# Pair 0's products with v begun inside the bias network, and pair 1's first tiles placed ahead of pair 0's last two

## The chip, the core and the metric

The kernel runs on one core of one Trainium2 chip. The metric is the device time of one launch in microseconds (us), from the start of the program to its end. Engines are named as the profile names them: PE is TensorE's matmuls and PEld its weight loads, DVE is VectorE, ACT is ScalarE, POOL is GpSimd, SP is SyncE, whose queue issues nearly all DMAs.

## What is computed

The reference is an attention with a bias made by a small network, followed by a two-layer mixer. Cut to what matters here:

```python
scores = scale * np.matmul(q, k.transpose(0, 1, 3, 2))          # (4, 8, 576, 576), head size 64
x = (psi_rel / psi_i)[..., None]                                # (576, 576, 1): from positions alone
h = np.maximum(x @ w1 + b1, 0.0)                                # 32 hidden values for each pair of positions
bias = h @ w2                                                   # (576, 576, 8): one plane for each head
scores = scores + bias.transpose(2, 0, 1)[None]
attn = np.exp(scores - np.max(scores, axis=-1, keepdims=True))
attn = attn / (np.sum(attn, axis=-1, keepdims=True) + 1e-09)
out = np.matmul(attn, v)                                        # then: u = x + mix(x); u + relu(u @ w1) @ w2
```

## The kernel before

**Two parts matter here: the bias network, and the attention of the 16 pairs that follows it.** A pair `p` is two heads of one batch (4 batches, 4 pairs in each). The last half of the program, the mixer, is not touched.

**The bias network** is the loop at L792, one turn `i` for each of 36 row tiles `T` (16 rows of the bias each), in the order of L786: the four tiles of rows 512 to 575 first, then tiles 0 to 31. In turn `i`, `bias_hid` (L299) makes the four hidden blocks of tile number `i`, mostly one on ACT (L308) and three on DVE (L310). `bias_mm` (L320) then multiplies the hidden blocks of the tile made two turns earlier with w2 on PE (L328), in strips of 32 columns of the array, and `bias_out` (L339) scales the result on ACT (L342) and writes it to DRAM by a DMA (L345). The hidden blocks live in a ring of 12 (three tiles), the scaled results in a ring of 6, and the PSUM tiles tagged `s` in three banks, which scores share. `bias_loads` (L352) reads the finished bias back in the layout of a head pair: `(c, hp)` is row block `c` (0 to 3, or 4 for the last 64 rows) of pair `hp`; `BIAS_AT` and the list `loads` say when.

**A pair** has nine tiles of scores, `s` = 0 to 8. `scores` (L376) puts q k into PSUM (L399), four matmuls of 288 columns, eight for `s` = 0, which holds the last 64 rows of both heads. `minima` (L403) adds the bias and takes the row minimum on DVE (L407), `exps` (L422) is the exponential on ACT (L425). `tr` (L465) transposes a tile on PE (L472) and copies it out as `pt`, `tr_m` (L475) does so for the 64 rows of `s` = 0, `tr_mid` (L484) for the middle columns. `av` (L498) multiplies v with `pt` into one PSUM bank (L508): ten matmuls over 320 columns for the first half `hf` = 0, over 256 for the second. `assemble` (L519) turns the result and scales it. `slot` (L581) puts all of that in order for tile `s` of pair `p`, together with what is left of pair `p` - 1: its last transposes, its second `av`, its `assemble`.

**Pair 0 begins inside the network.** `early` (L788) places the scores of its tiles 0 to 3 in turns 20, 23, 26 and 30; `minima` comes a turn later and the rest of the slot two turns later. Its other five tiles follow the network, then pair 1 and so on, in the loop at L866. The engines are in-order queues: what stands ahead in the program goes first.

**Operands.** q and k are held as two parts each whose sum has full precision: `hi` is the rounded value, and the difference to it goes to the lower half of `hi` for q and to `lo` for k. `prep_ops` (L173) makes them; from pair 1 on this is POOL's work, and POOL does not start it before the last hidden block of the network is written (the copy at L798 waits for it).

## Time and profile before

| | us |
|---|---|
| time, median of 3 runs | 729.47 (728.37 to 730.01) |
| profiled execution, its own time | 727.51 |
| its span, first to last instruction | 725.70 |
| PE busy | 707.5 (97%) |
| DVE busy | 537.1 (74%) |
| ACT busy | 402.9 (56%) |
| POOL busy | 273.1 (38%) |

The span is what the trace shows; the profiled execution is 1.81 us longer than its span, and 1.96 us shorter than the median. The times in brackets in the trace are how long an engine sat idle before an instruction and what released it. A matmul's end is modelled, so the pace of PE is read from the starts, above all from those of the weight loads (PEld). A float32 matmul shows as two records: the ten matmuls of one `av` are 20.

### The profile page before, as it was taken

The numbers are of one execution on the slowest core, as the hardware profiler recorded it, in microseconds if no ns is written. First come the engines' busy times: TensorE is split into PE (matmuls) and PEld (weight loads), VectorE is DVE, ScalarE is ACT, GpSimd is POOL, SyncE is SP. The second block draws the span as 40 slices with busy tenths as digits, with TensorE's granted clock in tenths as the row PEclk, the third lists the DMA queues.
The fourth block names the chain that finished last, engine by engine and source line by source line (L and its number), as shares of the span: only waits on it lengthen the run. The fifth ranks groups of instructions, "written<-read, shape, count | busy, mean of one in ns | idle before, by whom it ended". The sixth has DMA issues, their size and how long they took to land.

```text
span 725.7 us, 13129 instructions
## 1 busy us (share of the span) xinstructions
PE 707.5 (97%) x4620; PEld 561.2 (77%) x4620; DVE 537.1 (74%) x1202; ACT 402.9 (56%) x915; POOL 273.1 (38%) x287
## 2 busy tenths in 40 slices
PE   6999999999999999999999999999999999999997
PEld 2547888788777877878787888888787788888886
DVE  7985688788787777656658689999999953655545
ACT  7897778788778778864223335555555421222220
POOL 0006967567655557701150323536436300000000
PEclk9999999999999999999999999999999999999999
DMA  6889984565565546522293504637434665633313
GB/s 204 272 312 294 304 230 117 140 184 159 140 176 156 144 122 183 182 97 88 74 355 128 206 29 153 217 135 275 149 117 160 239 259 180 256 125 122 155 58 117
DMA packets 53393, 127.19 MB, mean 175 GB/s; under 512 B 8784, under 2 KB 12368, under 8 KB 52048
## 3 DMA queue, kind: packets, MB, share of 16 engines
q1 hardware_dynamic: 53088, 126.10, 53.1%
q8 instruction: 37, 0.61, 0.4%
q10 hardware_dynamic: 240, 0.26, 0.1%
q14 instruction: 28, 0.23, 0.1%
HBM read 81.34 MB, written 44.99 MB: 174 GB/s over the span
## 4 chain that ended last, share of the span: by engine, by line
PE 74%; ACT 9%; DVE 9%; issue 3%; DMA 2%; POOL 2%; SPq 0%; DVEq 0%; POOLq 0%; ACTq 0%
PE po L1334 15%; PE sb L1273 12%; PE o L508 11%; PE sc L399 10%; PE ph L676 7%; PE tb L472 7%; PE po L701 5%; PE bs L328 2%; ACT p L425 1%; POOL wy L266 1%; DVE acc L1320 1%; ACT pt L452 1%; ACT ring L308 1%; PE ph L1362 1%; ACT ring L342 1%
## 5 line engine op out<-in xcount | busy, mean ns | idle before, releaser
L1320 DVE TENSOR_TENSOR acc<-po,acc 128x512 f32<-128x512 f32 x108 | 74.1, 687 | 50.5 <-PE po L1334 44.1
L425 ACT ACTIVATE p<-p,st 128x576 f32<-128x576 f32 x128 | 99.9, 781 | 11.0 <-DVE st L407 10.6
L407 DVE CUSTOM_DVE_ANT_0 p<-sc,bias 128x576 f32<-128x576 f32 x128 | 95.9, 751 | 9.2 <-DMA bias<-bias_dram 4.7
L266 POOL TENSOR_TENSOR wy<-wt,wy 128x256 int32<-128x256 int32 (+1 forms) x68 | 50.3, 740 | 135.4 <-DVE wt L261 118.4
L399 PE MATMUL sc<-hi 128*128 128x288 f32 x320 | 100.6, 331 | 0.1
L399 PE MATMUL sc<-lo,hi 128*128 128x288 f32 x320 | 89.1, 295 | 0.0
L508 PE MATMUL o<-pt,v 128*64 128x320 f32 (+1 forms) x640 | 85.4, 411 | 0.1
L472 PE MATMUL tb<-ident,p 128*128 128x128 f32 x512 | 78.3, 275 | 1.4 <-DVE pt L454 0.9
L1334 PE MATMUL po<-wq,hq 128*128 128x512 f32 x288 | 73.5, 391 | 0.5 <-DVE ut L1367 0.5
L399 PEld LDWEIGHTS sc<-hi 128*128 128x128 f32 x320 | 60.3, 189 | 11.5 <-issue 8.0
L472 PEld LDWEIGHTS tb<-ident,p 128*128 128x128 f32 x512 | 59.8, 140 | 10.9 <-issue 7.6
L508 PEld LDWEIGHTS o<-pt,v 128*64 128x64 f32 x640 | 44.4, 136 | 30.1 <-issue 3.0
L452 ACT COPY pt<-tb 128x512 f32<-128x512 f32 x88 | 51.3, 582 | 23.4 <-PE tb L472 23.2
L1334 PEld LDWEIGHTS po<-wq,hq 128*128 128x128 f32 x288 | 53.5, 188 | 12.6 <-DVE ut L1367 0.9
L399 PEld LDWEIGHTS sc<-lo,hi 128*128 128x128 f32 x320 | 60.6, 189 | 0.5
L1273 PE MATMUL sb<-ut,w1q 128*128 128x512 f32 x216 | 55.1, 390 | 0.4 <-ACT acc L1277 0.3
L1273 PE MATMUL sb<-ut,wq 128*128 128x512 f32 x216 | 55.0, 390 | 0.5 <-ACT acc L1277 0.4
L328 PE MATMUL bs<-ring,small_sb 128*32 128x512 f32 (+48 forms) x640 | 43.8, 400 | 9.2 <-ACT ring L308 6.7
L701 PE MATMUL po<-w2q,hh 128*128 128x512 f32 x216 | 52.2, 393 | 0.4 <-DVE x_sb L576 0.4
L1334 PE MATMUL po<-w2q,ut 128*128 128x512 f32 x180 | 49.1, 389 | 0.0
L676 PE MATMUL ph<-ut,w1q 128*128 128x512 f32 (+1 forms) x240 | 48.2, 351 | 0.5 <-DVE ut L646 0.5
L1277 ACT COPY acc<-sb 128x512 f32<-128x512 f32 x48 | 28.0, 583 | 36.5 <-PE sb L1273 36.3
(153 smaller groups left out, 1447.6 us busy)
## 6 DMA issues: line engine op xcount, KB each, us to landing
wraw<-in_w_ch_dram SPq DMA_DIRECT2D x64, 256.0 KB, 3.4
raw<-in_qk_dram SPq DMA_DIRECT2D x50, 304.0 KB, 4.1
bias_dram<-ring SPq DMA_DIRECT2D x30, 296.0 KB, 3.9
acc<-u_dram SPq DMA_DIRECT2D x26, 256.0 KB, 4.6
ub_dram<-ut SPq DMA_DIRECT2D x12, 512.0 KB, 4.7
w_dram<-wq SPq DMA_DIRECT2D x12, 512.0 KB, 4.5
ut<-ub_dram SPq DMA_DIRECT2D x12, 512.0 KB, 4.3
v<-in_vp_dram SPq DMA_DIRECT2D x16, 320.0 KB, 3.0
```

The costliest lines, as they stand in the source:

```text
L328: mm(bs[T][32 * cg : 32 * cg + 32, o + a : o + e], lhsT=w2_sb, rhs=hid[:, far + left - e : far + left - a][:, ::-1] if a >= left else hid[ ...
L399: mm(ps[:, a, 0:HALF], lhsT=hi[:, q0 : q0 + P], rhs=kk, start=(i == 0), stop=(i == n - 1))
L407: nc.vector.tensor_tensor_reduce(out=halves(d["dst"]), in0=d["ps"][:, :, 0:HALF], in1=halves(bias[hp][:, s * S : (s + 1) * S]), scale=-0.1 ...
L425: nc.scalar.activation(out=dst, in_=dst, func=AF.Exp, bias=st[:, s : s + 1], scale=-1.0, accum_out=st[:, 10 + s : 11 + s])
L452: nc.scalar.copy(out=out, in_=in_)
L472: nc.tensor.transpose(bank[:, kb, :], src[:, b0 + kb * P : b0 + (kb + 1) * P], ident)
L508: mm(o[hd * D : (hd + 1) * D, 0:n], lhsT=v[:, vb * D : (vb + 1) * D], rhs=pt[:, pb, :], start=(j == 0), stop=(j == 4),)
L676: mm(st["ps"][:, f, :], lhsT=w, rhs=x, start=(i == 0), stop=(i == 3 * KD - 1))
L701: mm(ps, lhsT=h, rhs=w, start=(m == 0), stop=(m == 3 * nf - 1))
L1273: mm(bank[b], lhsT=w[:, c, r, :], rhs=u[:, r, :], start=first and i == 0, stop=i == 5, skip_group_check=True)
L1320: nc.vector.tensor_tensor(out=a, in0=ps, in1=a, op=ALU.add)
L1334: mm(ps, lhsT=h, rhs=w[:, r, :], start=m == 0, stop=m == 5)
```

## The change

Line numbers in the diff are those of before. Seven things are changed together:

1. **Pair 0 inside the network.** `early` moves its tiles 0 to 2 to turns 18, 21 and 24, its tile 3 to turn 33, and tile 4 joins in turn 36. `tr_m` is put in turn 24, the transposes of row block 0 in turns 26 and 28, the first part of `tr_mid` in turn 30. In turns 31 to 35 the first `av` runs on columns 0 to 191 (`LEFT + P`), two matmuls in each turn. The bank `o00` stays open; the other 128 columns follow after the network.
2. **The order after the network** is now the list `turns_at`: pair 0's tiles 4, 5, 6, pair 1's tile 0, the rest of pair 0's first `av`, pair 1's tiles 1 and 2, pair 0's tiles 7 and 8, then pair 1 from tile 3. Pair 0's leftover work moves to pair 1's tiles 3 to 6.
3. **Pair 1's operands.** q is loaded once and not twice; POOL makes `hi` of k, `hi` of q and the difference of q; the difference of k (`lo`) goes to DVE, ahead of pair 0's `minima` of tile 5.
4. **Loads.** Bias `(4, 1)`, k of pair 2 and v of pairs 0 and 1 are loaded inside the network; the order of the bias loads after it is `(0, 1)`, `(1, 1)`, `(3, 0)`, then the rest.
5. **Pair 2's operands**: k before q. 
6. **Start**: the two constants `sgn` and `eps` are set by POOL, and the scaling of `psi_sb` goes from DVE to ACT.
7. **Room**: a fourth tile `p` of scores; the sixth result buffer `e5` lies in a part of pair 1's bias that is loaded last.

```diff
-BIAS_AT = {9: (4, 0), 17: (0, 0), 25: (1, 0), 33: (2, 0)}
+BIAS_AT = {9: (4, 0), 12: (4, 1), 17: (0, 0), 25: (1, 0), 33: (2, 0)}
...
-    pp = p1.enter_context(tc.tile_pool(name="pp", bufs=3, side="left"))
+    pp = p1.enter_context(tc.tile_pool(name="pp", bufs=4, side="left"))
...
-        return [lambda: part(0, 0, QKW), lambda: part(D, LEFT, QKW), lambda: part(D, 0, LEFT)]
+        return [lambda: part(0, 0, K0), lambda: part(0, K0, QKW), lambda: part(D, K0, QKW)]
...
+            if p == 1:
+
+                def low_k():
+                    for a in range(0, K0, n):
+                        nc.vector.tensor_tensor(
+                            out=lo[:, a : a + n], in0=raw[:, K0 + a : K0 + a + n],
+                            in1=kh[:, a : a + n].bitcast(F32), op=ALU.subtract,
+                        )
+
+                return [lambda: copy_(kh, raw[:, K0:QKW]), *q_ops, low_k]
...
-    e5 = tabp.tile([P, S + LINE], F32, name="e5")
+    e5 = bias[1][:, 7 * S : 8 * S + LINE]
+    nc.gpsimd.memset(sgn.bitcast(F32), -2.0)
+    nc.gpsimd.memset(eps, 1.0e-9)
...
-    nc.vector.tensor_scalar(out=psi_sb, in0=psi_sb, scalar1=b1_sb, scalar2=None, op0=ALU.mult)
+    nc.scalar.activation(out=psi_sb, in_=psi_sb, func=AF.Copy, scale=b1_sb)
...
-        if old and s == (AV_OLD if new else AV_LAST):
+        if old and s == (5 if first else AV_OLD if new else AV_LAST):
             av(p - 1, 1)
-        if old and s == 0:
+        if old and s == (3 if first else 0):
             tr(p - 1, 3, 0, "a")
-        elif old and s == 1:
+        elif old and s == (4 if first else 1):
...
-    early = {20: 0, 23: 1, 26: 2, 30: 3}
+    early = {18: 0, 21: 1, 24: 2, 33: 3, 36: 4}
...
-        if i == 30:
-            load_v(0)
+        if i in (6, 20):
+            load_v(i > 6)
+        if i == 16:
+            loads.append(load_once(2)[1])
...
+        if i == 22:
+            recip(0, 0)
+        if i == 24:
+            tr_m(0, "a")
+        if i == 26:
+            tr(0, 0, 0, "d")
+        if i == 28:
+            tr(0, 0, 1, "d")
+        if i == 30:
+            tr_mid(0, 0, "d", 0)
+            o00 = av_bank()
+        if 31 <= i < 36:
+            av_mm(0, 0, o00, 0, LEFT + P, (i - 31,))
...
-    for c, hp in ((4, 1), (3, 0), (0, 1)):
-        loads += bias_loads(c, hp)
-    loads += load_once(2) + bias_loads(1, 1) + bias_loads(2, 1) + [lambda: load_v(1)] + bias_loads(3, 1) + load_once(3)
+    loads += bias_loads(0, 1) + bias_loads(1, 1) + bias_loads(3, 0) + [load_once(2)[0]]
+    loads += bias_loads(2, 1) + bias_loads(3, 1) + load_once(3)
...
+    prep = prep_ops(1)
+    for _ in range(3):
+        prep.pop(0)()
+    turns_at = [(0, 4), (0, 5), (0, 6), (1, 0), (0, None), (1, 1), (1, 2), (0, 7), (0, 8)]
+    turns_at += [(p, s) for p in range(1, NP) for s in range(9) if p > 1 or s > 2]
+    for p, s in turns_at:
+        if s is None:
+            av_mm(0, 0, o00, LEFT + P, LEFT + 2 * P)
+            av_out(0, 0, o00, LEFT + 2 * P)
+            continue
...
+        if (p, s) == (0, 5):
+            prep.pop(0)()
```

What this does to the queues, at three places. PE, in the network's turns 32 and 33, before (`tb` is a bank of transposes, `bs` the network's result; two rows of `bs` are one tile):

```order
L472 MATMUL tb<-ident,p 128x128 x4
L328 MATMUL bs<-ring,small_sb 32x447 x4
L328 MATMUL bs<-ring,small_sb 32x144 x4
L328 MATMUL bs<-ring,small_sb 32x463 x4
L328 MATMUL bs<-ring,small_sb 32x128 x4
```

PE in the turns 30 to 33, after (`ti` is the bank of the middle columns, `o` the open bank of `av`):

```order
L507 MATMUL ti<-ident,p 128x128
L510 MATMUL ti<-ident,pm 128x128
L343 MATMUL bs<-ring,small_sb 32x415 x4
L343 MATMUL bs<-ring,small_sb 32x176 x4
L522 MATMUL o<-pt,v 64x192 x2
L343 MATMUL bs<-ring,small_sb 32x431 x4
L343 MATMUL bs<-ring,small_sb 32x160 x4
L522 MATMUL o<-pt,v 64x192 x2
L343 MATMUL bs<-ring,small_sb 32x447 x4
```

Where PE had only the network's own products, it now turns to other work and back once in nearly every turn.

DVE at the network's end, before (the `ring` row is the last hidden tile, `fold` and `rep` small constants for the mixer, L407 is `minima`):

```order
L310 TENSOR_SCALAR ring<-wtab,small_sb 128x512 x3
L829 TENSOR_TENSOR fold<-ident 128x64
L830 TENSOR_TENSOR rep<-fold 128x96
L836 TENSOR_TENSOR rep<-fold 128x32
L407 ISA p,st<-sc,bias_109 128x576
```

DVE at the same place, after (`minima` is L422 here, and the first one shown is pair 0's tile 4):

```order
L325 TENSOR_SCALAR ring<-wtab,small_sb 128x512 x3
L422 ISA p,st<-sc,bias_109 128x576
L422 ISA st 128x1
L869 TENSOR_TENSOR fold<-ident 128x64
L870 TENSOR_TENSOR rep<-fold 128x96
L876 TENSOR_TENSOR rep<-fold 128x32
L218 TENSOR_TENSOR lo<-raw,hi 128x608 x2
L422 ISA p,st<-sc,bias_109 128x576
```

The two subtractions for `lo` of pair 1 now stand between pair 0's `minima` of tiles 4 and 5.

POOL from its first copy on, before:

```order
L798 TENSOR_SCALAR warm<-ring 128x1
L184 TENSOR_SCALAR hi<-raw 128x1216
L192 TENSOR_TENSOR hi<-raw,hi 64x608 x2
L184 TENSOR_SCALAR hi<-raw 128x1216
L192 TENSOR_TENSOR lo<-raw,hi 128x608 x2
```

POOL at the same place, after:

```order
L824 TENSOR_SCALAR warm<-ring 128x1
L200 TENSOR_SCALAR hi<-raw 128x1216
L200 TENSOR_SCALAR hi<-raw 64x1216
L204 TENSOR_TENSOR hi<-raw,hi 64x608 x2
L460 TENSOR_SCALAR pm<-praw,st 128x576
```

The pair of subtractions for `lo` has left POOL; the copy of k now comes first.

## Rows read from the trace of the kernel before

**Rows 1.** The page's chain of work that ended last, shares by engine.
```profile
PE 74%; ACT 9%; DVE 9%; issue 3%; DMA 2%; POOL 2%; SPq 0%; DVEq 0%; POOLq 0%; ACTq 0%
```

**Rows 2.** Busy time by stretch: engines, clock, DMA share, GB/s; network's second half, then after.
```profile
31.00:57.00 26.00, 24.42 (x316) 11.86 (x310) 22.62 (x67) 23.92 (x45) 1.51 (x3) 1.00 0.90 306
57.00:82.50 25.50, 25.37 (x192) 19.78 (x191) 15.38 (x43) 19.28 (x48) 19.56 (x16) 1.00 0.97 299
```

**Rows 3.** Timeline, PE's weight loads in the network: start, length, engine, line, [idle before].
```profile
37.35 0.67 PEld L328 LDWEIGHTS bs<-ring,small_sb 128*32 128x32 f32 x16 [0.17 <-issue]
...
38.87 1.16 PEld L328 LDWEIGHTS bs<-ring,small_sb 128*32 128x32 f32 x24 [0.85 <-ACT ring L342]
...
41.00 0.19 PEld L399 LDWEIGHTS sc<-hi 128*128 128x128 f32 x1 [0.41 <-issue]
...
41.72 0.16 PEld L328 LDWEIGHTS bs<-ring,small_sb 128*32 128x32 f32 x8 [0.16 <-issue]
...
43.97 0.16 PEld L328 LDWEIGHTS bs<-ring,small_sb 128*32 128x32 f32 x8 [1.50 <-ACT ring L342]
...
56.59 0.19 PEld L399 LDWEIGHTS sc<-hi 128*128 128x128 f32 x1
```

**Rows 4.** Chain that ended last, in order of time, after the network: start, length, what.
```profile
79.77 2.84 PE o L508 x20
...
86.56 2.36 PE o L508 x20
...
89.51 0.53 PE sc L399 x4
90.04 0.22 PE tx L526 x2
...
90.37 0.44 PE tb L472 x4
```

**Rows 5.** Timeline, the start of the network.
```profile
4.48 0.29 DVE L294 TENSOR_SCALAR small_sb<-small_sb 128x144 f32<-128x144 f32 x1
...
4.81 2.03 ACT L308 ACTIVATE ring<-wtab,small_sb 128x528 f32<-128x528 f32 x3 [1.18 <-DVE eps L783]
```

**Rows 6.** Timeline: a result of the network, two copies for pair 0, a `minima`.
```profile
36.34 0.76 ACT L342 ACTIVATE ring<-bs,small_sb 128x591 f32<-128x591 f32 x1 [0.33 <-DMA bias_dram<-ring]
...
51.04 0.69 DVE L454 COPY pt<-tb 128x512 f32<-128x512 f32 x1 [0.58 <-PE tb L472]
...
59.33 0.65 ACT L452 COPY pt<-tm 128x256 f32<-128x256 f32 x2
...
64.69 0.76 DVE L407 CUSTOM_DVE_ANT_0 p<-sc,bias 128x576 f32<-128x576 f32 x1 [3.32 <-DMA bias<-bias_dram]
```

**Rows 7.** Timeline, operands of a pair, and PE's first scores of pairs 1 and 2.
```profile
22.12 1.42 DVE L192 TENSOR_TENSOR lo<-raw,hi 128x1216 fp32r<-128x1216 f32 x1
...
55.41 0.29 POOL L798 TENSOR_SCALAR warm<-ring 128x1 f32<-128x1 f32 x1 [54.53 <-ACT ring L308]
...
56.95 2.95 POOL L192 TENSOR_TENSOR hi<-raw,hi 64x608 fp32r<-64x608 f32 x2
...
65.57 0.19 PEld L399 LDWEIGHTS sc<-hi 128*128 128x128 f32 x1 [0.59 <-issue]
...
82.54 0.19 PEld L399 LDWEIGHTS sc<-hi 128*128 128x128 f32 x1 [0.49 <-issue]
```

**Rows 8.** Timeline later on: DVE beside POOL.
```profile
101.82 2.99 POOL L204 TENSOR_TENSOR hi<-raw,hi 64x608 fp32r<-64x608 f32 x2
...
103.49 1.46 DVE L255 TENSOR_SCALAR wt<-wt 128x256 int32<-128x256 int32 x1
```

**Rows 9.** Line L255 in the whole trace: ns, min/median/max.
```profile
L255 DVE TENSOR_SCALAR wt<-wt x68: 243/294/1459, 96.9 to 578.1; 128x256 int32<-128x256 int32 x66, 128x160 int32<-128x160 int32 x1, 128x128 int32<-128x128 int32 x1
```

**Rows 10.** Chain that ended last, in order of time: two pieces of DMA.
```profile
28.79 7.46 DMA bias_dram<-ring
...
61.67 2.90 DMA bias<-bias_dram
```

More of the change, by code (lines that the diff above doesn't have):

```diff
@@ L482, in tr_m, with tr_mid @@
             copy(eng, pt[:, 5 * hd : 5 * hd + 4, 0:LEFT], bank[:, :, hd * LEFT : (hd + 1) * LEFT])
-    def tr_mid(p, hf, eng):
+    def tr_mid(p, hf, eng, part=None):
         pt = get_pt(p, hf)
@@ L487, in tr_mid, with av_mm @@
         bank = psum("t", [P, 4, P], "ti")
-        for i in range(2):
+        which = range(2) if part is None else (part,)
+        mixed = hf == 0 and part != 1
+        for i in which:
             nc.tensor.transpose(bank[:, i, :], d["P"][2 * hf + i][:, 4 * P : 5 * P], ident)
         o = LEFT if hf == 0 else 0
-        if hf == 0:
+        if mixed:
             nc.tensor.transpose(bank[:, 2, :], d["pm"][:, 4 * P : 5 * P], ident)
-        copy(eng, pt[:, 4, o : o + 2 * P], bank[:, 0:2, :].rearrange("p a b -> p (a b)"))
-        if hf == 0:
+        a, e = which[0], which[-1] + 1
+        copy(eng, pt[:, 4, o + a * P : o + e * P], bank[:, a:e, :].rearrange("p a b -> p (a b)"))
+        if mixed:
             copy(eng, pt[0:LEFT, 4, 0:LEFT], bank[0:LEFT, 2, 0:LEFT])
             copy(eng, pt[LEFT:P, 4, 0:LEFT], bank[LEFT:P, 2, LEFT:P])
-    def av(p, hf):
-        d = pair[p]
-        pt = d["pt", hf]
-        n = 320 if hf == 0 else 256
-        v = v_t[p]
-        o = psA.tile([P, 512], F32, tag="a", name="o")
-        for j in range(5):
+    def av_mm(p, hf, o, a, e, js=range(5)):
+        pt, v = pair[p]["pt", hf], v_t[p]
+        for j in js:
             for hd in range(2):
@@ L583, in slot @@
         new, old = p < NP, p > 0
+        first = p == 1
         if new and not begun:
@@ new lines @@
+        if (p, s) == (CONV_FROM[0], 0):
+            queue += by_twos(jobs)
+        if s == 8 and 0 < p < HP - 1:
+            loads += late
+        n = 2 if p else 3
+        for o in loads[0:n]:
+            o()
+        del loads[0:n]
+        if p % HP == 0 and p and s == 8:
+            mix_t(p // HP - 1)
+        slot(p, s, begun=(p, s) == (0, 4))
+        background(int(s in conv_at and (p, s) >= CONV_FROM))
+        if p > HP and p % HP == 1:
+            for c in {2: (4, 0), 3: (1,), 4: (2,), 5: (3,)}.get(s, ()):
+                mix_h(p // HP - 1, c)
```

135 lines of the change are left out of this document (64 added, 71 removed).

## The prediction

> **What bounds the kernel now.** I read the shares of the chain that ended last first: PE holds 74% of it, no other engine 10% [rows 1]. The pairs' and the mixer's time is the sum of PE's instructions, so whatever PE does earlier shortens the program by that much, if PE does not wait for it elsewhere. Then the stretches. After the network PE is busy for 25.37 of 25.50 us; in its second half for 24.42 of 26.00, with ACT at 23.92 and DVE at 22.62 [rows 2]: three engines near their limit, none of them full. Busy PE is modelled, so I took the weight loads for the true pace. They show PE waiting inside the network for ACT's results, 0.85 us before 38.87 and 1.50 us before 43.97 [rows 3]. That is the room the change wants to use. The first scores of pair 2 start at 82.54 [rows 7]; from there on before and after run almost the same work in the same order (pair 2's operands are only made in another order), so I make the sum up to that instruction.
>
> **The change part by part.**
>
> *Start.* DVE's scaling of psi (0.29 us from 4.48) stands ahead of the first hidden blocks at 4.81 [rows 5]. It goes to ACT, which is idle there for 1.18 us, and the constants to POOL, idle too. The first hidden block then waits for the table alone, 0.2 us earlier. I take -0.2; at worst ACT's own scaling takes as long and nothing is won.
>
> *The network's length on PE.* Two tiles and the turn to scores take 2.13 us, from 38.87 to 41.00 [rows 3]: 1.0 a tile and some 0.13 for the turn. The visit to scores, 41.00 to 41.72, is 0.72 for four matmuls worth 0.53 [rows 3, 4], so the way back is 0.19 and a visit costs about 0.3 beside its work. From 37.35 to 56.59 PE does 14 tiles (14.0), two visits for scores and one for transposes (1.50 of work, 0.44 for four transposes [rows 4], and 0.9 of turns): 16.4 of 19.24, so 2.8 us of idle time [rows 3, 4].
> Added in these turns: one tile of scores 0.53, one `tr` 0.44, `tr_m` 0.44, two single transposes 0.22 [rows 4], and the first part of `av`. No row shows `av` at 192 or 128 columns; 20 records take 2.84 us at 320 columns and 2.36 at 256 [rows 4], 0.0075 us a column, so the line gives 1.88 at 192 and 1.40 at 128. Work added: 3.5. Visits: ten in place of three (the `av` of turn 33 follows scores directly), seven more. At 0.3 they cost 2.1, at nothing 0; no row shows a turn between `av` and the network's strips, so I take 0.25, between the two and near the row: 1.75. Together 5.25, less the 2.8 of idle: the network ends 2.4 us later, if all idle time is used and ACT and DVE keep up. Ends: 0.7 with free visits; 3.8 if half of the idle time stays.
> ACT gets the copies of `tr_m`, 0.65; DVE one copy of 0.69, the smaller ones of `tr_mid` (no more than that) and one `minima` of 0.76 [rows 6], some 2.1. In 26 us they have 2.1 and 3.4 to spare [rows 2]; the exponentials and the scaling of `pm` move to where ACT waits now. I cost them at nothing, with PE's longer turns as cover; without it DVE's share is up to 2.1, not on top of PE's but in place of it.
> The Trainium skill speaks against this part: its page "TensorEngine Tiling (Array Packing)", section "Tiling Modes", says that a change of tiling mode drains TensorE. By it the turns between 64-column `av` and 32-column strips cost what the shown ones do, and the network's end would come 2.7 us later, not 2.4; the rows show the gap of 0.13 to 0.19 only between full-width work and strips.
>
> *What PE has left after the network.* Gone: 0.53 + 0.44 + 0.44 + 0.22, and 2.84 - 1.40 = 1.44 of `av`: 3.1 us less. The split itself costs 0.44.
>
> *PE's waits after the network.* Before, from 56.59 to 82.54, PE's work is 24.0 of 25.95 (13 `tr`, 2 `tr_m`, 13 score tiles at 0.53 and one at 1.06, `av` 2.84 twice and 2.36, 13 single transposes at 0.11), so 1.9 idle. Of this 0.59 stands before pair 1's scores at 65.57 [rows 7]: the last bias rows were read until 64.57 [rows 10], and DVE waited 3.32 us for them [rows 6]. With pair 1's three tiles ahead, this read has until pair 0's tile 7 to arrive: -0.6.
> A new wait takes its place: pair 1's operands. POOL's first copy starts behind the last hidden block; warm and one copy take 1.54 us (55.41 to 56.95) and the difference 2.95 [rows 7]; with the second copy of about 1.25 that is 5.7. Hidden blocks are written two turns ahead, so about 2.4 before the network's end on PE; POOL is done 3.3 after it, where PE, with two score tiles, two `tr` and a transpose (2.1) and two short waits for ACT and DVE, arrives at about 2.6: +0.7. The fold and rep operations and the two subtractions for `lo` (1.42 for both [rows 7]) stand on DVE ahead of `minima` of tile 5, whose PSUM bank pair 1's scores need. With DVE undisturbed they end before POOL, +0. Beside a busy POOL they may wait: a DVE operation with a median of 0.294 us [rows 9] took 1.46, until POOL's second subtraction ended [rows 8]. At worst each waits for one POOL instruction, +1.7; I take +0.3, nearer to no wait, since POOL has only its last subtractions left when they come up.
>
> *Loads.* The order of issue puts (4,1), v(1) and k of pair 2 into the network and takes pair 1's second copy of q out. That is about 0.6 MB more there, 2.1 us at the 306 GB/s of [rows 2]. One write of the network took 7.46 us to land [rows 10], and ACT waited 0.33 us for it [rows 6]. As PE sets the turns now, I take 0, with 2.1 as the other end.
>
> **The sum.** -0.2 + 2.4 - 3.1 - 0.6 + 0.7 + 0.3 = -0.5 us at pair 2's first scores, and no row shows a reason why later work should take it back. Against the profiled execution, 727.51 - 0.5 = 727.0; the median stands 1.96 above that execution, so 729.0.
>
> **The rivals.**
>
> *A. Faster: the visits are free.* If PE takes up `av` and transposes without a gap, the network grows by 0.7 and not 2.4, and the `lo` operations wait for nothing: -0.5 - 1.7 - 0.3 = -2.5, thus 727.0, down to 726.3 if the wait for POOL vanishes too. For it: 20 records of `av` are followed by scores at 82.54 without a gap (79.77 + 2.84 is 82.61) [rows 4, 7], and several of the network's waits are ACT's, not PE's. Against it: 41.00 to 41.72 [rows 3].
>
> *B. Slower: DVE is held up by POOL.* Each of fold, rep and `lo` then ends behind a POOL instruction, pair 1's first scores start 1.7 later and PE has nothing in front of them in its queue: -0.5 + 1.4 + 0.7 (every visit at 0.35) = +1.6, thus 731.1. It decides the sign once those scores start more than about 0.5 us later than in my sum. For it: [rows 8, 9]. The Trainium skill has this as a rule: "SBUF — State Buffer", section "Who interferes with whom", says that a DVE instruction with two SBUF inputs and a GpSimd instruction that reads SBUF exclude each other for its whole length. The trace agrees, with 1.46 against 0.294. Against it: POOL is through with most of its work before DVE gets there.
>
> *C. Slower: the network waits for its DMAs.* The 0.6 MB delay writes and the bias of row block 0, `minima` and ACT stand still for up to 2.1: 730.5 to 731.1. For it: the wait at 36.34 [rows 6]; against it: it is 0.33 us now.
>
> *D. The change does not do what it says:* PE is full in the network, and the products only lengthen it by what they save later. That is what most of my own sum is, 2.4 against 3.1; it ends in the forecast.
>
> **How the numbers follow.** About 0.2%, or 1.5 us, is what a measurement of this kernel can tell from no change. Forecast with D, within 0.2%: 0.39. A: 0.36, faster. B: 0.15 and C: 0.10, slower. The range reaches from A's end, 726.3, to B and C with a little of both, 731.4; it leaves out two or more mishaps at once.
>
> **What would show it.** Right: weight loads in turns 31 to 35 at a distance of 1.5 us, with a gap of 0.1 to 0.2 at each turn; the last network product about 2.2 us later than 56.5, near 58.8; pair 1's first scores near 62 with a wait for POOL or DVE; pair 2's first scores within 1.5 us of 82.54. A is right if the network ends before 57.5; B if a `lo` subtraction takes over 1 us and pair 1's scores start after 63.5; C if ACT waits for `bias_dram` writes or `minima` of tile 1 for its bias. The sum is wrong if pair 2's first scores move otherwise than the time does: then something behind them has changed, which I cost at nothing.

## The result, and the profile after

The changed kernel takes **735.20 us** (median of 4 runs, 733.93 to 736.13) against 729.63 (4 runs beside it): ratio 1.0078, with a 95% interval of 1.0057 to 1.0099. It is 5.7 us slower, outside the range of the prediction. Its profiled execution took 734.69 us, span 732.9.

The profiled execution of before (727.51) lies 2 us under its own median, that of the changed kernel does not. So single traces of one kernel can differ by 2 us, more than most versions below do from each other, and a cause counts as shown only where ratios show it. One thing holds in all 20 traces: the profiled time is the start of pair 2's first scores plus 644.5 to 646 us (before: 82.54 and 645.0; after: 89.36 and 645.3). So all that was lost or won in these traces lies ahead of them.

The two stretches of [rows 2] in the trace of the changed kernel (length, then busy time and count of PE, PEld, DVE, ACT and POOL, granted clock, DMA share, GB/s):

```profile
31.00:57.00 26.00, 24.04 (x290) 11.60 (x294) 21.70 (x67) 21.80 (x41) 0.00 (x0) 1.00 0.90 304
57.00:82.50 25.50, 23.13 (x203) 17.42 (x196) 15.84 (x38) 16.92 (x38) 13.78 (x13) 0.93 0.83 247
```

In the network, which was to become denser, PE is busy for 24.04 us instead of 24.42, and DVE and ACT for less too. Behind 57 PE stands idle for 2.4 us (0.1 before), and its clock is no longer 1.00. Four places stand out. First the network's turns 18 to 22, on DVE (start, busy us, instruction, and in brackets the idle time before it and what ended that):

```profile
39.70 0.76 DVE L422 CUSTOM_DVE_ANT_0 p<-sc,bias 128x576 f32<-128x576 f32 x1 [3.23 <-DMA bias<-bias_dram]
```

and in SP's queue of transfers, same columns:

```profile
30.99 1.13 SPq L164 DMA_DIRECT2D raw<-in_qk_dram  x1
32.17 0.84 SPq L380 DMA_DIRECT2D bias<-bias_dram  x1
```

The `minima` of pair 0's tile 1 wait 3.23 us for bias (0,0). Its read is issued at 32.17 (30.59 before), right behind the moved load of pair 2's k. Second, the network's last turns, PE's weight loads (they answer to [rows 3]):

```profile
57.77 0.20 PEld L522 LDWEIGHTS o<-pt,v 128*64 128x64 f32 x4 [0.20 <-issue]
58.25 0.16 PEld L343 LDWEIGHTS bs<-ring,small_sb 128*32 128x32 f32 x8 [0.28 <-issue]
...
59.86 0.16 PEld L343 LDWEIGHTS bs<-ring,small_sb 128*32 128x32 f32 x8 [0.28 <-issue]
...
61.73 0.16 PEld L343 LDWEIGHTS bs<-ring,small_sb 128*32 128x32 f32 x8 [0.17 <-issue]
...
62.86 0.19 PEld L414 LDWEIGHTS sc<-hi 128*128 128x128 f32 x1
```

A turn with a visit takes 1.61 us (58.25 to 59.86) without an idle gap: 1.0 for the tile, 0.38 for the visit's work (a fifth of 1.88), so 0.23 for the turn. The network's last product begins at 61.73 (55.46 before) and the next load follows at 62.86 (56.59). Third, behind the network, DVE:

```profile
62.52 1.00 DVE L869 TENSOR_TENSOR fold<-ident 128x64 f32<-128x64 f32 x1
63.55 1.45 DVE L870 TENSOR_TENSOR rep<-fold 128x96 fp32r<-128x96 f32 x1
...
65.03 1.48 DVE L218 TENSOR_TENSOR lo<-raw,hi 128x608 fp32r<-128x608 f32 x2
66.43 0.74 DVE L422 CUSTOM_DVE_ANT_0 p<-sc,bias 128x576 f32<-128x576 f32 x1
```

POOL in the same stretch:

```profile
59.50 2.38 POOL L200 TENSOR_SCALAR hi<-raw 128x1216 fp32r<-128x1216 f32 x2
61.95 2.94 POOL L204 TENSOR_TENSOR hi<-raw,hi 64x608 fp32r<-64x608 f32 x2
```

and PE's weight loads behind it:

```profile
67.30 0.19 PEld L414 LDWEIGHTS sc<-hi 128*128 128x128 f32 x1 [2.19 <-issue]
...
68.70 2.00 PEld L522 LDWEIGHTS o<-pt,v 128*64 128x64 f32 x20 [0.28 <-DVE pt L469]
```

While POOL writes pair 1's operands, fold and rep take 1.00 and 1.45 us. In before's trace, where POOL began its first copy only at 55.66, they were 0.22 and 0.26; DVE there:

```profile
55.13 0.22 DVE L829 TENSOR_TENSOR fold<-ident 128x64 f32<-128x64 f32 x1
55.39 0.26 DVE L830 TENSOR_TENSOR rep<-fold 128x96 fp32r<-128x96 f32 x1
```

In the changed kernel fold ends at 63.52 and rep at 65.00, rep right behind POOL's last subtraction (64.89). The `lo` subtractions and tile 5's `minima` come behind them, pair 1's first scores wait for the bank that these free, and PE stands idle for 2.19 us ahead of them (0.59 before, [rows 7]). Fourth, what follows, in stretches of 2 us, with the columns of the first fence:

```profile
64.00:66.00 2.00, 1.35 (x10) 0.92 (x9) 2.00 (x4) 0.53 (x2) 0.89 (x1) 1.00 0.65 191
66.00:68.00 2.00, 0.67 (x5) 0.70 (x6) 2.00 (x5) 0.78 (x3) 0.00 (x0) 1.00 1.01 339
68.00:70.00 2.00, 2.00 (x17) 1.72 (x17) 1.43 (x5) 1.75 (x5) 0.00 (x0) 0.58 1.01 340
70.00:72.00 2.00, 2.00 (x17) 1.67 (x14) 0.00 (x0) 1.20 (x4) 0.00 (x0) 0.57 1.04 301
```

After the idle stretch the granted clock falls to 0.57, near the lower level of 1.2 GHz, for some 4 us. The 20 loads of the rest of the product with v then take 2.00 us; at the full clock (e1) they take 1.11.

### The profile page after: what moved, and what is told of

It reads as the page before. It is cut to its first block, busy times and chain, and to the rows that moved or that the text cites. A ratio compares the mean times of both kernels' runs of the same rounds, so it can differ in the third digit from the quotient of the medians.

```text
span 732.9 us, 13171 instructions
## 1 busy us (share of the span) xinstructions
PE 711.6 (97%) x4640; PEld 563.7 (77%) x4640; DVE 541.1 (74%) x1203; ACT 403.6 (55%) x915; POOL 269.5 (37%) x287
## 4 chain that ended last, share of the span: by engine, by line
PE 74%; DVE 10%; ACT 7%; DMA 4%; POOL 3%; issue 2%; SPq 1%; DVEq 0%; POOLq 0%; ACTq 0%
PE po L1383 15%; PE sb L1322 12%; PE o L522 11%; PE sc L414 10%; PE tb L487 7%; PE ph L704 5%; PE po L729 4%; PE bs L343 4%; POOL wy L279 1%; DVE acc L1369 1%; PE ph L1411 1%; ACT p L440 1%; DMA u_dram<-acc 1%; ACT pt L467 1%; DMA bias<-bias_dram 1%
## 5 line engine op out<-in xcount | busy, mean ns | idle before, releaser
L422 DVE CUSTOM_DVE_ANT_0 p<-sc,bias 128x576 f32<-128x576 f32 x128 | 95.8, 751 | 13.7 <-PE sc L414 9.3
L522 PE MATMUL o<-pt,v 128*64 128x256 f32 (+3 forms) x660 | 87.1, 409 | 0.0
L522 PEld LDWEIGHTS o<-pt,v 128*64 128x64 f32 x660 | 46.6, 139 | 29.2 <-issue 3.9
L343 PE MATMUL bs<-ring,small_sb 128*32 128x512 f32 (+47 forms) x640 | 45.4, 408 | 8.7 <-ACT ring L323 6.8
```

The costliest lines, as they stand in the source:

```text
L343: mm(bs[T][32 * cg : 32 * cg + 32, o + a : o + e], lhsT=w2_sb, rhs=hid[:, far + left - e : far + left - a][:, ::-1] if a >= left else hid[ ...
L422: nc.vector.tensor_tensor_reduce(out=halves(d["dst"]), in0=d["ps"][:, :, 0:HALF], in1=halves(bias[hp][:, s * S : (s + 1) * S]), scale=-0.1 ...
L522: mm(o[hd * D : (hd + 1) * D, a:e], lhsT=v[:, vb * D : (vb + 1) * D], rhs=pt[:, pb, a:e], start=(j == 0), stop=(j == 4),)
```

## The experiments

All ratios are to the kernel before, timed beside each run. "End" is the start of the network's last product (the last tile's), "pair 2" that of pair 2's first scores, both from one trace each. Where a row joins the last tile's loads with earlier ones (f4), its last load stands in for it, 59.51, less the 0.88 us between the two in before.

| run | ratio (95%) | end | pair 2 |
|---|---|---|---|
| changed kernel | 1.0078 (1.0057–1.0099) | 61.73 | 89.36 |
| e1 fold later | 1.0075 (1.0053–1.0096) | 61.90 | 91.16 |
| e2 pair 2's k later | 1.0059 (1.0042–1.0075) | 60.47 | 88.00 |
| e3 no visits | 1.0087 (1.0071–1.0102) | 59.69 | 91.56 |
| e4 = e1 + e2 | 1.0048 (1.0033–1.0063) | 60.30 | 88.30 |
| e5 = e4, (3,0) first | 1.0047 (1.0032–1.0061) | 60.00 | 87.32 |
| e6 order mended | 1.0064 (1.0047–1.0081) | 61.26 | 90.71 |
| e7 = e6, pairs in order | 1.0050 (1.0035–1.0065) | 62.28 | 88.55 |
| e8 bias (0,0) early | 1.0050 (1.0030–1.0069) | 61.33 | 88.63 |
| f1 = e5, no round trip | 1.0060 (1.0041–1.0079) | 60.32 | 87.86 |
| f2 before, no round trip | 1.0006 (0.9993–1.0019) | 56.07 | 84.41 |
| f3 part two alone | 1.0011 (0.9998–1.0025) | 56.59 | 85.97 |
| f4 before, five products | 1.0010 (0.9995–1.0026) | 58.63 | 85.88 |
| g1 = e5, pair 1's bias early | 1.0022 (1.0012–1.0032) | 59.96 | 85.68 |
| g2 = f3, pair 1's bias early | 0.9996 (0.9987–1.0006) | 55.98 | 85.07 |
| g3 before, pair 1's bias early | 1.0022 (1.0013–1.0031) | 56.18 | 85.94 |
| g4 all mended | 1.0021 (1.0012–1.0030) | 60.91 | 86.43 |
| h1 = g2, pair 2's k early | 1.0021 (1.0011–1.0032) | 56.79 | 85.89 |
| h2 before, tiles early | 0.9991 (0.9981–1.0002) | 57.23 | 84.31 |

### Rivals B and C, and the visits: e1 to e4

```diff
-    nc.vector.tensor_tensor(out=fold, ...)
+        if (p, s) == (1, 4):
+            make_rep()                          # e1
...
-        if i == 16:
-            loads.append(load_once(2)[1])       # e2; the load goes to the end of the list
...
-        if 31 <= i < 36:
-            av_mm(0, 0, o00, 0, LEFT + P, (i - 31,))
-            av_mm(0, 0, o00, LEFT + P, LEFT + 2 * P)
+            av_mm(0, 0, o00, 0, LEFT + 2 * P)   # e3, behind pair 1's first scores
```

**e1.** 

> The changed kernel (735.2) with one edit: the three VectorE operations that build fold and rep, which only the mixer reads much later, stand behind pair 1's tile 4 instead of right behind the bias network. Theory B (VectorE held behind fold and rep while GpSimd writes pair 1's operands: 1.00 + 1.45 + 0.18 us at 62.52, then lo, then tile 5's minima at 66.43, on which pair 1's first scores wait until 67.33): lo starts near 62.7, the minima near 64.2, pair 1's first scores near 65.0 where GpSimd's last subtraction ends (64.89), so 2.3 us earlier; TensorE has no idle stretch ahead of them, its granted clock stays 1.00 in 66 to 72, and a further 1.5 to 2 us come from that. About 731.2, between 730.5 and 732.0. Rival (the wait is GpSimd's, VectorE's queue only stands beside it, and what follows is paced by the loads): pair 1's first scores move by under 0.8 us, the clock still falls to 0.57: 734.4 to 735.2.

Nothing was won (735.14). `lo` now stands where fold stood, and the same two instructions take 3.55 us instead of 1.48, POOL's 3.47 instead of 2.94. e1's DVE:

```profile
62.69 3.55 DVE L218 TENSOR_TENSOR lo<-raw,hi 128x608 fp32r<-128x608 f32 x2
66.17 0.75 DVE L422 CUSTOM_DVE_ANT_0 p<-sc,bias 128x576 f32<-128x576 f32 x1
...
74.97 0.76 DVE L422 CUSTOM_DVE_ANT_0 p<-sc,bias 128x576 f32<-128x576 f32 x1 [3.05 <-DMA bias<-bias_dram]
```

and its POOL:

```profile
62.12 3.47 POOL L204 TENSOR_TENSOR hi<-raw,hi 64x608 fp32r<-64x608 f32 x2
```

So B's mechanism is real, but fold was only the first to meet it. PE's product with v did run at the full clock:

```profile
68.30 1.11 PEld L522 LDWEIGHTS o<-pt,v 128*64 128x64 f32 x20 [0.16 <-DVE st L422]
```

Its second tile of pair 1 began at 69.58 instead of 71.04, and the next wait took it all: tile 7's `minima` for bias (3,0), 3.05 us. This kernel's clock fell there instead.

**e2.** 

> The changed kernel (735.2) with one edit: the load of pair 2's k (issued at 30.99, 1.13 us on SP's queue, 1216 columns by 64 rows) goes back behind the bias network. Theory C in the form that the load is late: the read of bias (0,0) is issued at 31.0 instead of 32.17 and finds less traffic; the 3.23 us wait of tile 1's minima at 39.70 falls to under 1.5; the network's end and all behind it come 1.5 to 2.5 us earlier: 732.7 to 733.7. Rival (the tile stands too early: it was moved two turns ahead of its bias, and the read takes its 7.4 us whatever is issued before it): the wait stays above 2 us, and the time above 734.2. Second rival (the network is bound by TensorE from turn 28 on and swallows the wait): the wait shrinks and the last product of the network stays within 0.4 of 61.73.

The wait fell from 3.23 to 2.19 us only, as the rival says, and the time by 1.5 us, as theory C says. But the intervals of e2 and the changed kernel overlap, so this needed h1.

**e3.** 

> The changed kernel (735.2) without the five visits of pair 0's product with v in the network's last turns: all five blocks over 320 columns run in one piece where the rest of it stood, behind pair 1's first scores; everything else as changed. Theory (the late turns are bound by TensorE, and each visit costs its whole 0.48 us there): the network's last product starts at 59.0 to 59.5 instead of 61.73, the piece behind it takes 2.84 instead of 1.4 us at the full clock: in all 0.8 to 1.2 us faster, 734.0 to 734.4. Rival, as the prediction had it (visits fit into TensorE's idle time but for about 0.25 us each): the last product moves by under 1.3 us, and the kernel is 0.2 us slower or more: 735.4 to 736.2.

The end came 2.0 us earlier, 0.41 a visit, but PE then waited longer for pair 1's operands (3.76 us), and the whole product with v ran at the low clock. Nothing was won: behind the network an earlier end is worth nothing while `lo` and the `minima` behind it (65.96, against 66.43 in the changed kernel) set the time. PE's load of pair 1's first scores in e3:

```profile
66.83 0.29 PEld L414 LDWEIGHTS sc<-hi 128*128 128x128 f32 x1 [3.76 <-issue]
```

**e4.** 

> The first two edits together: fold and rep behind pair 1's tile 4, pair 2's k loaded behind the network. If both causes are real and lie on the path one behind the other, their gains add (4.0 and 2.0): 729.0, that is level with the kernel before (729.6), between 728.2 and 730.2. If one swallows the other, it is as fast as the better of the two alone (731.2).

733.10: a little better than e2 alone (not resolved by the intervals), far from the sum. The gains do not add.

### Bias (3,0), the order of the tiles, bias (0,0): e5 to e8

```diff
-    loads += bias_loads(0, 1) + bias_loads(1, 1) + bias_loads(3, 0) + ...
+    loads += bias_loads(3, 0) + bias_loads(0, 1) + bias_loads(1, 1) + ...   # e5, e6, e7
...
-        if (p, s) == (0, 5):                    # e6, e7
+        if (p, s) == (0, 6):
             prep.pop(0)()
...
+    turns_at = [(0, 4), (0, 5), (0, 6), (0, None), (1, 0), (1, 1), (1, 2), (0, 7), (0, 8)]   # e6
+    turns_at = [(0, 4), (0, 5), (0, 6), (0, None), (0, 7), (0, 8), (1, 0), (1, 1), (1, 2)]   # e7
...
-BIAS_AT = {9: (4, 0), 12: (4, 1), 17: (0, 0), ...
+BIAS_AT = {9: (4, 0), 12: (4, 1), 15: (0, 0), ...                           # e8
```

**e5.** 

> The kernel with fold and rep behind pair 1's tile 4 and pair 2's k loaded behind the network (733.1), with one more edit: bias (3,0), which pair 0's last two tiles read, stands ahead of pair 1's bias (0,1) and (1,1) in the list of loads behind the network, not behind them. Theory (with the VectorE block out of the way the bias read is the next thing late: tile 7's minima waited 2.09 us for it at 72.43, TensorE 1.62 at 73.25): both waits go, about 731.3, between 730.6 and 732.0. Rival (pair 1's bias is then the late one, its tiles being the first to be read): a wait of the same size at pair 1's second tile, 732.7 to 733.5.

The rival was right, 733.48. The wait only changed its owner: on DVE pair 1's tile 1 follows pair 1's tile 0, and it waits for (0,1). That row of e5's DVE:

```profile
70.14 0.76 DVE L422 CUSTOM_DVE_ANT_0 p<-sc,bias 128x576 f32<-128x576 f32 x1 [2.85 <-DMA bias<-bias_dram]
```

f1 and f2 below were built on reading this row as tile 7 waiting for (3,0), which it is not.

**e6.** 

> The changed kernel (735.2) with four edits of order alone: fold and rep behind pair 1's tile 4; bias (3,0) first of the loads behind the network; VectorE's subtractions for pair 1's lo behind pair 0's tile 6 instead of ahead of tile 5; the rest of the product with v ahead of pair 1's first scores. Pair 2's k stays where the change put it. Theory (VectorE's subtraction can't run while GpSimd's runs, 3.55 us against 1.48 with the same operands; so whatever stands behind it on VectorE waits, and TensorE with it): lo starts where GpSimd ends (65.6) and takes 1.5, nothing but pair 1's scores stands behind it, TensorE does the rest of the product in the meantime, pair 1's first scores at about 67.1 and the second tile's at 67.9 (69.58 with fold alone moved), clock 1.00 throughout: 729.5 to 731.0. Rival (the subtraction takes its time whatever runs beside it, or the scores wait for something else): first scores later than 68, 732 or more.

`lo` behind POOL took 1.48 us again, the first scores came at 66.75, as expected; but pair 1's tile 1 then waited for (0,1) until 71.35 and the clock fell behind that wait (0.50 in 72 to 76). 734.96: not a mend by itself.

**e7.** 

> The same kernel as e6_rest_first but for the order of the tiles: pair 0's last two tiles stand ahead of pair 1's first three, as they did before the change. What it tells: whether pair 1's tiles ahead are worth anything once the queue on VectorE is mended. Theory (pair 1's operands are GpSimd's 6.1 us behind the network's end, so pair 1's first scores can't be earlier than about 67 in either order, and pair 0's two tiles are the cover for that): as fast as e6 within 0.7, or faster. Rival (the order of the change is what hides the bias read of (3,0)): tile 7's minima wait for it by more than 1.5 us, and the kernel is over 1.0 us slower than e6.

733.66, 1.3 us less than e6, though the intervals overlap. No gain of pair 1's tiles ahead shows here; tile 7 waited 1.54 us for its bias, so the rival's wait is there, and its price is not.

**e8.** 

> The changed kernel (735.2) with one number changed: the read of bias (0,0) stands two turns earlier, turn 15 instead of 17, so ahead of the last load of pair 1's operands and of pair 2's k. Theory (the tile was moved ahead of its bias, and the k load is only a third of the wait: without it 3.23 fell to 2.2): the wait of tile 1's minima falls under 0.8 us, the network's last product starts at 59.0 to 59.8 instead of 61.73, 732.0 to 733.2. Rival (TensorE bounds the network anyway and swallows it): the last product not before 60.6, 733.7 or more.

Tile 1's `minima` on DVE in e8:

```profile
37.30 0.76 DVE L422 CUSTOM_DVE_ANT_0 p<-sc,bias 128x576 f32<-128x576 f32 x1 [0.23 <-DMA bias<-bias_dram]
```

The wait of 3.23 us shrank to 0.23, yet the end moved by 0.4 only: the network swallows most of it, as the rival said. The time, 733.87, is lower than the changed kernel's, but the intervals overlap.

### Where the trip through DRAM does not count: f1 and f2

```diff
-            in1=halves(bias[hp][:, s * S : (s + 1) * S]),
+            in1=halves(bias[hp][:, (s - 2 * (p == 0 and s > 6)) * S :][:, 0:S]),
```

**f1.** 

> The kernel with fold and rep moved, pair 2's k loaded late and bias (3,0) first (733.5), with one more edit: the minima of pair 0's tiles 7 and 8 read the columns of tiles 5 and 6's bias, which have long been there, not bias (3,0). This leaves the right bias of those two tiles out; the read of (3,0) is still issued and lands as before. New theory T: the time is the network's end, plus the trip of the table's last rows through DRAM (last product, ACT's eviction, write, read: 61.30 to 70.14 there, and 56.76 to 64.69 in the kernel before), plus the work behind it; TensorE's idle 1.77 and 2.16 us are that trip showing, because the change took into the network what used to lie beside it. Then the second idle stretch goes, 730.8 to 731.8. Rival (the stretch is paced by VectorE and GpSimd, and the trip only stands beside it): 732.9 to 733.6.

**f2.** 

> The kernel before (729.6) with the same edit: tiles 7 and 8 of pair 0 read older bias columns. This leaves the right bias of two tiles out. Theory T: in the kernel before the trip is nearly covered (8.1 us of work on TensorE between the network's end and 65.57), so it is worth only the short idle stretches of TensorE ahead of tile 7's transposes (0.16, 0.51, 0.39 at 69.69 to 72.69): 728.5 to 729.3. Rival (the trip is as open in the kernel before as in the changed one, so that it explains nothing of the difference): 727.0 to 728.0.

Neither gained (733.88 and 729.70). In f1 the wait stands as it did, 3.07 us, because it is pair 1's; theory T, that the last rows' trip sets the time, found no support. f1's DVE:

```profile
70.65 0.76 DVE L422 CUSTOM_DVE_ANT_0 p<-sc,bias 128x576 f32<-128x576 f32 x1 [3.07 <-DMA bias<-bias_dram]
```

### Each part alone, and a visit's price: f3 and f4

The first part of the change is the work inside the network, the second the order behind it.

```diff
-    early = {18: 0, 21: 1, 24: 2, 33: 3, 36: 4}
+    early = {20: 0, 23: 1, 26: 2, 30: 3}        # f3: and no tr, tr_m, tr_mid, av in the network
...
+        if 31 <= i < 36:                        # f4, in the kernel before
+            for hd in range(2):
+                mm(idle[hd * D : (hd + 1) * D, 0:192], lhsT=ident[:, 0:D], rhs=tab[:, 0:192], ...)
```

**f3.** 

> The second part of the change alone, with its queues mended: the network as before the change (tiles 0 to 3 in turns 20, 23, 26 and 30, no transposes or products with v in it), and behind it pair 1's first three tiles ahead of pair 0's last two; fold and rep behind pair 1's tile 4, bias (3,0) the first of the loads, VectorE's lo behind tile 6, pair 2's k late. Theory T: the network ends at 56.5 as before, and the trip of (3,0) is covered by pair 0's tiles, the whole first product with v and pair 1's three tiles; pair 2's first scores 0.5 to 1.5 us earlier than in the kernel before (82.54): 728.0 to 729.2. Rival (pair 1's tiles ahead cost by themselves, by their bias reads and operands): 730.2 or more.

730.55, in the rival's range, with 1 inside the interval of the ratio: no gain of the second part shows. PE waited 0.56 us ahead of pair 1's tile 2 and 1.31 ahead of pair 0's tile 7, the second time because pair 1's tile 1 held its bank while its `minima` waited 1.10 us for bias (0,1).

**f4.** 

> The kernel before (729.6) with five idle visits added in the network's turns 31 to 35, each as large as one of the change's first visits (two products of 64 by 192 columns, of the identity with the table; nobody reads the result). What a visit costs where it delays the network's end, with nothing else changed. Theory T (each delays the end by its whole 0.4 to 0.5 us, and the end's delay is the kernel's delay): 731.5 to 732.2. As the prediction had it, 0.25 us each: 730.8. Rival A of the prediction (TensorE's idle time in the network takes them in): 729.4 to 730.0.

730.56, or 0.7 us above before with an interval of -0.4 to 1.9, which leaves out theory T's time. Its first half holds in the trace all the same. From the scores of pair 0's tile 3 (turn 30) to the network's last load, PE takes 9.25 us before, in f2 too, whose network is the same:

```profile
47.09 0.19 PEld L399 LDWEIGHTS sc<-hi 128*128 128x128 f32 x1 [0.30 <-ACT p L425]
...
56.34 0.13 PEld L328 LDWEIGHTS bs<-ring,small_sb 128*32 128x32 f32 x4 [0.30 <-issue]
```

and 11.45 in f4:

```profile
48.06 0.19 PEld L399 LDWEIGHTS sc<-hi 128*128 128x128 f32 x1 [0.30 <-ACT p L425]
...
59.51 0.13 PEld L328 LDWEIGHTS bs<-ring,small_sb 128*32 128x32 f32 x4 [0.30 <-issue]
```

Five visits are 2.4 us of PE's time and delay the network's end by 2.2, or 0.44 each (e3: 0.41). Its idle time takes up 0.2 of them. How much of the delay reaches the kernel's end, the ratio is too wide to tell.

### The reads of pair 1's bias: g1 to g4

```diff
-BIAS_AT = {..., 25: (1, 0), 33: (2, 0)}
+BIAS_AT = {..., 25: (1, 0), 28: (0, 1), 30: (1, 1), 33: (2, 0)}
...
-    loads += bias_loads(3, 0) + bias_loads(0, 1) + bias_loads(1, 1) + ...
+    loads += bias_loads(3, 0) + ...
```

**g1.** 

> The kernel with fold and rep moved, pair 2's k late and (3,0) first (733.5), with one more edit: pair 1's bias (0,1) and (1,1) are read inside the network, at turns 28 and 30, and not behind its end. New theory D: behind the network the tiles wait for reads, of whichever bias stands last in the list: they are issued in one row behind the network's last write (nine reads from 64.30 on), while the DMA engines were 0.46 and 0.65 busy in 60 to 68 and are full (0.96 and more) from 68 on; the 2.85 us wait at 70.14 was pair 1's tile 1 for (0,1). With two of the three reads made in the network (0.82 busy in 40 to 60) that wait and TensorE's 2.16 us go: 730.6 to 731.9. Rival (the engines are full in sum, and a read made early only delays another): a wait of 1.5 us or more for another bias, or a longer network; 732.8 or more.

731.57, inside the expected range. In 68 to 72 PE is busy for 3.68 us (e5: 2.08); pair 1's tile 1 starts its `minima` at 68.49 with no wait for a read. The stretch by engines (columns as in the first fence), e5:

```profile
68.00:72.00 4.00, 2.08 (x17) 1.84 (x16) 1.80 (x6) 1.84 (x7) 0.82 (x2) 1.00 0.96 291
```

and g1:

```profile
68.00:72.00 4.00, 3.68 (x29) 3.38 (x28) 3.35 (x9) 3.43 (x11) 1.37 (x3) 1.00 0.93 240
```

Pair 1's tile 1 on g1's DVE:

```profile
68.49 0.76 DVE L422 CUSTOM_DVE_ANT_0 p<-sc,bias 128x576 f32<-128x576 f32 x1 [1.25 <-PE sc L414]
```

The two intervals only touch (at 1.0032), and the wait named beforehand is gone: I count theory D as shown, 1.9 us.

**g2.** 

> Part two alone with its queues mended (730.55, against 729.3 for the kernel before) with the same edit. Theory D: the wait of pair 1's tile 1 (1.10 us at 68.46) and TensorE's 0.56 and 1.31 us ahead of it go: 728.8 to 729.6. Rival: as in the other run, a later read takes its place: 730.2 or more.

Ratio 0.9996, inside theory D's range (0.9993 to 1.0004 of the kernel before), but the interval overlaps f3's, so the edit's gain is not resolved here. In the trace the wait for (0,1) is gone; PE still waits 0.56 us ahead of pair 1's tile 2 and 0.47 ahead of pair 0's tile 8.

**g3.** 

> The kernel before (729.4) with this edit alone, pair 1's bias (0,1) and (1,1) read in the network's turns 28 and 30. Theory D: the 1.41 us wait at 72.21 goes, but TensorE is hardly idle there in the kernel before (0.16, 0.51, 0.39): 728.4 to 729.4. Rival (the early reads hold up the network's own): 729.8 or more.

Slower by 0.22%, in the rival's range. The rival's mechanism does not show: the network's end is at 56.18, against 56.07 in f2, whose network is untouched. Tile 7 now waits 3.65 us for (3,0) (3.32 before), and PE 1.34 ahead of pair 1's first scores (0.59). The same edit that saves 1.9 us in the changed kernel costs 1.6 in the kernel before; it is no gain of its own. Tile 7's `minima` on DVE in g3:

```profile
68.08 0.76 DVE L407 CUSTOM_DVE_ANT_0 p<-sc,bias 128x576 f32<-128x576 f32 x1 [3.65 <-DMA bias<-bias_dram]
```

**g4.** 

> The changed kernel (735.2) with all that the runs have named: bias (0,0) read at turn 15, pair 2's k late, (0,1) and (1,1) read in the network, (3,0) first behind it, fold and rep behind pair 1's tile 4, VectorE's lo behind tile 6, the rest of the product with v ahead of pair 1's first scores. What is left of the change's loss is then what the visits put on TensorE in the network. If the causes named are all: the network's last product at 59 to 60, no idle stretch of TensorE over 1 us behind it, 729.0 to 730.5, so level with the kernel before within 0.2 per cent. If 731.0 or more, one more cause is open.

1.0021, no better than g1. So one cause is left, and g2 says where: it differs from g4 only in having no first part and in the turn of one read, bias (0,0), and is 0.25% faster, with separate intervals. The first part itself costs about 1.8 us.

### Load or early tile: h1 and h2

```diff
+        if i == 16:
+            loads.append(load_once(2)[1])       # h1, in g2
...
-    early = {20: 0, 23: 1, 26: 2, 30: 3}
+    early = {18: 0, 21: 1, 24: 2, 30: 3}        # h2, in the kernel before
```

**h1.** 

> Part two alone with its queues and pair 1's bias mended (1.000 of the kernel before) with pair 2's k loaded at turn 16, as the change does it; pair 0's tile 1 stands where it stood before the change, its minima two turns later. Theory L (the wait of 3.23 us is the load and the early tile together; the load alone delays the read of bias (0,0) by the 1.1 us that SP takes for it, against a wait of 0.40 there now): the wait grows to 1.2 to 1.7 us and the kernel is 0.3 to 1.2 us slower, 1.000 to 1.002 of before. Rival (the load alone was the cause): wait 2.5 us or more and 1.002 or more. Second rival (as the prediction had it, loads cost nothing): wait as now, 0.4.

**h2.** 

> The kernel before (729.5) with pair 0's tiles 0, 1 and 2 at turns 18, 21 and 24 of the network, as in the change, not at 20, 23 and 26; tile 3 stays at 30 and nothing else changes, no load and no visit. Theory L: tile 1's minima come some 2.6 us earlier while their bias comes as before (ready without a wait there, at 37.8 at the latest): a wait of 1.0 to 2.5 us, of which the network's end, bound elsewhere by ACT's and TensorE's turns, gets 0.3 to 1.5: 729.8 to 731.0. Rival (the load alone was the cause): wait under 0.5 us, 729.0 to 729.8.

Tile 1's `minima` on DVE in h1:

```profile
39.42 0.76 DVE L422 CUSTOM_DVE_ANT_0 p<-sc,bias 128x576 f32<-128x576 f32 x1 [0.72 <-PE bs L343]
```

and in h2:

```profile
39.45 0.76 DVE L407 CUSTOM_DVE_ANT_0 p<-sc,bias 128x576 f32<-128x576 f32 x1 [2.28 <-PE bs L328]
```

The early tiles make a wait of 2.28 us that costs nothing that the ratio can tell (0.9991). The load makes hardly a wait (0.72; 0.40 in g2) and costs 0.25% against g2, some 1.8 us, with separate intervals. Of these two waits the more visible one was the free one. How the load costs its 1.8 us is not settled. The end and pair 2's first scores are both 0.8 us later than in g2's trace (56.79 against 55.98, 85.89 against 85.07), but as much is lost there before the load is issued: the network's 57th weight load stands at 10.62 against 9.85. So the ratio shows the price, and the traces show no place for it.

## Why the prediction was wrong

**Loads, 0 with an other end of 2.1.** The step failed. k of pair 2 alone costs 1.5 (e2) to 1.8 us (h1), near the other end; e2's part is not resolved. I had argued that PE sets the turns. It does in turns 31 to 35 (f4); ahead of them it still waits for ACT [rows 3]. Rival C named the loads; its sign, the wait of tile 1, came true, and by e8 and h2 it was not what cost. By which way the load costs is open.

**Bias (3,0), -0.6.** Failed, first of all as a reading of the row: 0.59 us of idle PE ahead of pair 1's first scores were put down to this bias. In f2, where no tile of pair 0 waits for it, 0.49 us still stand there:

```profile
66.30 0.19 PEld L399 LDWEIGHTS sc<-hi 128*128 128x128 f32 x1 [0.49 <-issue]
```

The same 0.49 us stand ahead of pair 2's first scores in 19 of the 20 traces (before's in [rows 7]). So 0.1 us was there to be won, not 0.6, and taking the trip away gained nothing in either kernel (f1, f2). The prediction also took only the read whose wait showed in [rows 6, 10] and not those that the change needs earlier: with pair 1's tiles ahead, (0,1) is due at 67 and is issued behind the network's last write. With the other waits gone, that was 1.9 us (g1 against e5).

**Pair 1's operands, +0.7, and DVE beside POOL, +0.3.** The first went to the wrong engine, the second was too small. POOL is done at 64.89, 2.0 us behind the network's end (62.86) and not 3.3, and before PE runs out of work at 65.11. DVE is what PE waits for, as rival B had it: 2.19 us of idle PE, 1.7 more than the 0.49 above, and 1.7 was the worst case that the prediction named and set aside. It let DVE come when POOL had "only its last subtractions left". Those two took 2.94 us, rep ended only behind them, and in e1 so did `lo` (66.24 against 65.59). The rule of the Trainium skill that B named ("SBUF — State Buffer", "Who interferes with whom") holds here: a DVE instruction with two SBUF inputs and a POOL instruction that reads SBUF exclude each other, and the trace agrees with 1.45 against 0.26 for rep, while `minima`, which reads PSUM and SBUF, kept its 0.76 us in the same stretch (62.01 in e1). The row that B gave for it, 1.46 against 0.294 [rows 8, 9], is no case of that rule: it has one tensor as input.

**The network's length, +2.4.** The visit's price was right: 0.25 assumed, 0.23 in the trace. What failed is "if all idle time is used". 2.35 of the 2.8 us stand at 38.87 and 43.97 [rows 3], ahead of turn 30, while the visits for the product with v come in turns 31 to 35; there f4 finds 0.2 us for them. In g1 the end is 4.0 us later than in g2, in g4 4.9, beyond the 3.8 for "half of the idle time stays". By the ratios the first part costs 1.8 us, which g4 could not mend; that the later end is the reason is likely and not shown by itself, since f4's time is not resolved. (The 2.7 that the prediction gives for turns at the shown price is 2.8 by its own terms, 3.5 + 2.1 - 2.8.)

**Work left, -3.1.** Came true as work and brought little time. From the network's last product to pair 2's first scores PE took 27.1 us before and 27.6 after; in g1, with its waits mended, 25.7.

**Start, -0.2.** Nothing, the bad end named there: ACT's own scaling waits for its data, and the first block starts at 4.83 (4.81 in [rows 5]). ACT in the changed kernel:

```profile
4.32 0.42 ACT L309 ACTIVATE small_sb<-small_sb 128x144 f32<-128x144 f32 x1 [0.68 <-DMA small_sb<-in_small_dram]
4.83 0.73 ACT L323 ACTIVATE ring<-wtab,small_sb 128x528 f32<-128x528 f32 x1
```

**The clock.** Not in the prediction at all. An idle stretch was priced at its length; where the clock falls behind it, PE pays again (2.00 us for loads worth 1.11, and the scores behind them).

**The range.** B and C were two rivals with a chance each, and the range left out "two or more mishaps at once". They are no independent mishaps: operands, bias reads and loads are all released by the network's end, which came 6.3 us later in the changed kernel's trace than in before's (0.9 of it from the start, see the last section). Several stood there side by side, each hiding the next, so that e1, e3 and e5 gained nothing, and only several mends together did: g1 is the first version of the whole change whose interval lies clear of the changed kernel's. Summed by ratios: 0.3% from k and fold (e4), 0.25% from pair 1's bias (g1), 0.2% from the first part. The share of k and fold is an estimate, as e4's interval still overlaps the changed kernel's. The first part has no mend here, and no version tried is faster than the kernel before by more than the measurement can tell (g2 and h2 are level with it).

## What to carry to other kernels

Before moving work ahead of a stage's end, list everything that the end releases (operands on another engine, reads that are queued behind its last write, buffers) with its own length: the work moved was their cover, and the longest of them is the new bound. A wait in a trace is a place, not a price: one of 2.28 us cost nothing (h2), and a load with hardly a visible wait cost 1.8 us (h1). The same holds for idle time: count only what lies in the turns where the new work will stand. When one mend gains nothing, look for the wait that took its place before dropping the theory, and try the mends together.
